# Feed-forward layer, first product: seven matmul products for eight on pairs of chunks and pairs of row blocks, with the weights' sums kept in DRAM

## The chip, the cores and the metric

The kernel runs on one core of a Trainium2 chip. A core has a matmul engine (TensorE, PE in the profile, with its weight loads as PEld), a vector engine (VectorE, DVE), a scalar engine (ScalarE, ACT), a general engine (GpSimd, POOL) and a queue engine (SyncE, SP) that issues most DMA transfers. Each engine runs its own list of instructions in order and waits on semaphores for the others. PE reads from on-chip memory (SBUF) and writes to eight accumulator banks of 128 x 512 floats (PSUM). The metric is the time of one execution on the device in microseconds; the number shown for a kernel is the median of its runs.

## What is computed

A linear attention, then a Fourier mixing, then a feed-forward layer on 8 x 576 = 4608 rows of 512 channels:

```
kv  = einsum('bhsd,bhse->bhde', k, v)
o   = einsum('bhsd,bhde->bhse', q, kv)
x   = o / sqrt(mean(o*o) + 1e-6) * g_norm
u   = x + real(fft(fft(x, seq), channels))
un  = (u - mean(u)) / sqrt(var(u) + 1e-6)
out = u + maximum(un @ w_ch1, 0) @ w_ch2
```

`w_ch1` is 512 x 2048 and `w_ch2` 2048 x 512, both in double precision in DRAM. The hidden width 2048 is cut into 16 chunks of 128, and the 4608 rows into 9 blocks of 512.

## The kernel before, in words

Every matmul of the feed-forward layer takes 128 x 128 stationary and 128 x 512 moving values. To keep float32 accuracy a value is split into a high and a low part, and a product is made of three passes (high x high, high x low, low x high). For one block and one chunk the first product takes 4 parts of the channels x 3 passes = 12 matmuls (`ffn1`, recorded at L469), and the second takes 4 row tiles x 3 passes = 12 matmuls (`ffn2`, L487). Between them ACT writes the high part of the relu (L479) and DVE the low part (L482).

The work has two stages. In the first, a planner (`Plan`) orders attention, Fourier part, and the feed-forward chunks 0 to 2 of all blocks (`plan_early`), whose sums go to the DRAM buffer `part_scr`; the transposed rows of `u`, split into high and low, go to `unT_scr`. The planner also prepares the weights of the first NA + NB1 = 7 chunks (`plan_w`). Preparing a weight chunk is a chain of DVE steps (L398 to L414, L1348, for `w_ch1` also L419 and L434), one ACT copy for the high part and one POOL subtraction for the low part.

In the second stage (from L1319) the list `segs` sets the order: the last four blocks first get chunks 3 to 6, with their sums in `next_scr`; then each block gets all the chunks that it lacks and is finished. Two loops run in it: over the segments, and in each over its chunks. Each pass of the inner loop issues the weight load of two passes ahead, `first` of this chunk, `second` of the pass before it, and the weight work of the next chunks (`sum_w`, `split_w`); when a block starts, the next block's `unT` is loaded (L1427). All prepared weights stay in SBUF. Near a block's end `load_parts` and `load_u` fetch the sums and `u`, compute the row scale (1 over the deviation) by bn_stats on DVE, and POOL adds the sums to `u` (L1418); the last chunk's accumulators are scaled, added and stored (L1456, L1461). The row scale is thus applied after both products: relu(a x) = a relu(x) for a > 0.

The instructions of this stage are not ordered by the planner but by a scheduler that works from the source's order and its own estimates, engine by engine. A tile of a pool that is used up, or whose memory another tile held before it, waits for the last reader of the old contents.

## Time and profile before

| | before |
| --- | --- |
| median of 3 runs | 1009.84 us (1007.83 to 1011.03) |
| span of the profiled execution | 1006.6 us |
| DVE busy | 488.3 us (49%) |
| ACT busy | 326.6 us (32%) |
| POOL busy | 322.2 us (32%) |
| HBM traffic | 139 GB/s over the span |

The table's lower part is from the profile's first part, the busy time of each engine in one profiled execution. Of that execution the profile gives the span from the first to the last instruction; the device time of the other runs holds a few microseconds more. In the views quoted below a row reads: line of the code, engine, operation, output tile <- input tiles, shapes, count, busy time, mean duration in ns. A row of the windows view gives, for a stretch of the span, the busy time of each engine with its count of instructions, then the granted clock of PE, the busy share of the DMA engines and what they moved.

### The profile page before, as it was taken

What the parts mean: (1) busy time and instruction counts of PE and PEld (TensorE: products, weight loads), DVE (VectorE), ACT (ScalarE), POOL (GpSimd) and SP (SyncE); (2) the same over time, 40 slices, a digit from 0 to 9 for tenths busy, and PEclk for the clock granted to TensorE, in tenths of its full rate; (3) what the DMA queues carried; (4) which work ended last, traced back from release to release, by engine and by line L of the source; (5) the groups of instructions that cost most, each with busy time, mean ns of one, the idle gap of its engine ahead of it and who ended that gap; (6) DMA issues with size and microseconds to landing.
All of it is one profiled execution on the core that took longest, in us unless ns stands there. A gap on an engine that the chain in (4) does not pass through costs nothing.

```text
span 1006.6 us, 15538 instructions
## 1 busy us (share of the span) xinstructions
PE 987.5 (98%) x6070; PEld 831.2 (83%) x6070; DVE 488.3 (49%) x946; ACT 326.6 (32%) x649; POOL 322.2 (32%) x338
## 2 busy tenths in 40 slices
PE   5999999999999999999999999999999999999998
PEld 4898889888878788888888888888888888888886
DVE  3588986778598689995131323221221311311212
ACT  2566655756544333444121212021021120210110
POOL 1557786785674132227440303020120020200000
PEclk9999999999999999999999999999999999999999
DMA  9889876873555865646642423320410400400101
GB/s 232 206 211 285 208 221 190 223 207 124 192 185 163 301 222 209 230 126 200 207 147 96 124 98 112 120 90 1 167 43 1 168 21 1 167 0 1 42 1 42
DMA packets 109405, 140.48 MB, mean 140 GB/s; under 512 B 51870, under 2 KB 77010, under 8 KB 104724
## 3 DMA queue, kind: packets, MB, share of 16 engines
q1 hardware_dynamic: 105652, 131.89, 42.9%
q0 software_dynamic: 1920, 6.29, 2.1%
q10 hardware_dynamic: 1760, 1.31, 0.5%
q8 instruction: 48, 0.79, 0.3%
q14 instruction: 25, 0.20, 0.1%
HBM read 88.07 MB, written 51.40 MB: 139 GB/s over the span
## 4 chain that ended last, share of the span: by engine, by line
PE 95%; DVE 3%; issue 1%; DMA 0%; POOL 0%; ACT 0%; DVEq 0%; POOLq 0%; ACTq 0%
PE ps_h L469 38%; PE acc L487 38%; PE ps_o L748 4%; PE ps_f L902 4%; PE ps_k L653 2%; PE ps_f L962 2%; PE ps_s L542 2%; PE ps_q L722 2%; PE ps_t L1063 1%; PE ps_w L428 1%; DVE x L853 1%; DMA raw<-in_moe_w_ch_dram 0%; DVE pm L991 0%; DVE ab L865 0%; DVE x L1007 0%
## 5 line engine op out<-in xcount | busy, mean ns | idle before, releaser
L469 PE MATMUL ps_h<-unTh,w 128*128 128x512 f32 x1152 | 356.6, 391 | 0.0
L487 PE MATMUL acc<-w,hh 128*128 128x512 f32 x1152 | 345.7, 391 | 0.0
L482 DVE SCALAR_TENSOR_TENSOR hl<-ps_h,hh 128x512 fp32r<-128x512 f32 x144 | 99.2, 689 | 376.3 <-ACT hh L479 372.1
L469 PEld LDWEIGHTS ps_h<-unTh,w 128*128 128x128 f32 x1152 | 215.0, 188 | 44.0
L487 PEld LDWEIGHTS acc<-w,hh 128*128 128x128 f32 x1152 | 214.6, 188 | 43.9 <-ACT unTh L1072 0.2
L479 ACT ACTIVATE hh<-ps_h 128x512 fp32r<-128x512 f32 x144 | 85.9, 597 | 475.5 <-PE ps_h L469 455.9
L469 PE MATMUL ps_h<-unTl,w 128*128 128x512 f32 x576 | 224.2, 389 | 0.0
L487 PE MATMUL acc<-w,hl 128*128 128x512 f32 x576 | 213.3, 390 | 0.0
L487 PEld LDWEIGHTS acc<-w,hl 128*128 128x128 f32 x576 | 108.1, 188 | 22.7
L469 PEld LDWEIGHTS ps_h<-unTl,w 128*128 128x128 f32 x576 | 108.0, 188 | 22.6
L1399 POOL DMA_INDIRECT uu<-u_scr,rowidx x24 | 23.4, 977 | 285.2 <-DVE uu L1456 177.6
L788 POOL TENSOR_TENSOR x<-x,gb 96x512 f32<-96x512 f32 (+1 forms) x42 | 53.7, 1299 | 32.9 <-ACT x L765 21.7
L1418 POOL TENSOR_TENSOR uu<-uu,up 128x512 f32<-128x512 f32 x36 | 45.7, 1295 | 45.7 <-ACT up L1415 45.7
L1362 POOL TENSOR_TENSOR w<-wap,w 128x512 fp32r<-128x512 f32 x18 | 23.3, 1295 | 70.0 <-ACT w L1361 70.0
L1456 DVE SCALAR_TENSOR_TENSOR uu<-acc,rs_yb,uu 128x512 f32<-128x512 f32 (+1 forms) x37 | 25.4, 730 | 41.1 <-PE acc L487 41.1
L748 PEld LDWEIGHTS ps_o<-kvt,fq 64*96 64x96 f32 (+1 forms) x864 | 38.9, 162 | 5.9 <-issue 1.4
L748 PE MATMUL ps_o<-kvt,fq 64*96 64x64 f32 (+1 forms) x864 | 42.2, 248 | 0.9 <-DVE x L853 0.6
L775 DVE TENSOR_REDUCE ss<-ps_o 96x8 f32<-96x512 f32 (+1 forms) x48 | 32.4, 685 | 21.7 <-ACT ps_o L770 21.6
L875 POOL TENSOR_TENSOR xe<-ab 96x256 f32<-96x256 f32 (+1 forms) x46 | 34.5, 770 | 25.6 <-DVE ab L865 22.6
L902 PE MATMUL ps_f<-cs,xh 96*128 96x290 f32 (+1 forms) x192 | 39.5, 300 | 0.0
L1406 DVE BATCH_NORM_STATS2 bst<-uu 128x6 f32<-128x512 f32 x36 | 24.5, 687 | 25.8 <-DMA uu<-u_scr,rowidx 17.6
L1075 DVE TENSOR_TENSOR unTl<-ps_t,unTh 128x384 fp32r<-128x384 f32 (+14 forms) x80 | 33.0, 472 | 2.8 <-ACT unTh L1072 2.8
(125 smaller groups left out, 1035.8 us busy)
## 6 DMA issues: line engine op xcount, KB each, us to landing
raw<-in_moe_w_ch_dram SPq DMA_DIRECT2D x32, 512.0 KB
unT_scr<-unTh SPq DMA_DIRECT2D x9, 1024.0 KB
unT_scr<-unTl SPq DMA_DIRECT2D x9, 1024.0 KB
part_scr<-part SPq DMA_DIRECT2D x36, 256.0 KB
unTh<-unT_scr SPq DMA_DIRECT2D x9, 1024.0 KB
unTl<-unT_scr SPq DMA_DIRECT2D x9, 1024.0 KB
up<-part_scr SPq DMA_DIRECT2D x36, 256.0 KB
out_dram<-uu SPq DMA_DIRECT2D x35, 256.0 KB
```

Of the source, the lines that this page charges most:

```text
L469: nc.tensor.matmul(ps, w[c][:, kc * P : (kc + 1) * P], unT[a][:, kc, :], start=(idx == 0), stop=(idx == 3 * KC - 1),)
L479: nc.scalar.activation(hh, ps, AF.Relu)
L482: nc.vector.scalar_tensor_tensor(hl, ps, 0.0, hh.bitcast(F32), ALU.max, ALU.subtract)
L487: nc.tensor.matmul(acc, hpair[a][:, i * P : (i + 1) * P], w[c], start=(first and n == 0), stop=(last and n == 2),)
L748: nc.tensor.matmul(pss[s].t[:n, at : at + D], fqs[side].t[half, m, :n], kvt.t[half, m], start=True, stop=True,)
L775: nc.vector.tensor_reduce(ss.t[0][:n, :, t, s::2], pss[s].t[:n].rearrange("p (u m e) -> p u m e", u=2, e=D), AX.X, ALU.add,)
L788: nc.gpsimd.tensor_tensor(v_, v_, gb[:n].unsqueeze(1).to_broadcast([n, H, D]), ALU.mult)
L875: nc.gpsimd.tensor_tensor(o[:, s], a[:, 0], a[:, 1], ALU.subtract if s else ALU.add)
L902: nc.tensor.matmul(ps.t[:, :NS], xs[t].t[a][:n, part, ch * P : (ch + 1) * P], cs[:n, part, c, t, :], start=(idx == 0), stop=(idx == 8),)
L1075: nc.vector.tensor_tensor(unTs[j].t[1][:, :, to], view()[:, :, lo:hi], unTs[j].t[0][:, :, to].bitcast(F32), ALU.subtract,)
L1418: nc.gpsimd.tensor_tensor(us[j][i], us[j][i], part, ALU.add)
L1456: nc.vector.scalar_tensor_tensor(ut[:, cols], acc_t[i][:, cols], scales[j][:, i : i + 1], ut[:, cols], ALU.mult, ALU.add,)
```

## The change

NB1 becomes 3: six chunks are prepared in the first stage, and all blocks do chunks 3 to 5 in the ordinary way in the second. Block 0 (`LONE`) alone does chunks 6 to 15 in the ordinary way, two at a time, between the segments of the other blocks. While that runs, the weights of chunks 6 to 15 are prepared in five groups of two. For each group the 512 x 256 piece of `w_ch1` is seen as 2 x 2 quarters of 256 channels x 128 hidden values; POOL makes four sums and differences of quarters (Winograd's form of Strassen's scheme), all are split into high and low, and the seven resulting operands go to `w1_scr` in DRAM, the `w_ch2` pieces to `w2_scr`.

Then all pools of the second stage are closed and a third stage begins, for the other eight blocks in four pairs. For a pair, `prep_u` fetches `u` of the two blocks and computes the row scale, `prep_z` loads high and low of `unT`, adds them and multiplies by the row scale (fetched through `scale_scr` so that it lies along the free axis), `prep_t` makes the four sums of the 2 x 2 quarters, `prep_b` splits the seven operands, and `prep_acc` adds the earlier sums to `u`. The main loop runs 4 pairs x 5 groups = 20 times. Each time it loads the group's weights again, does seven products of 6 matmuls (`mult`, two parts of the channels x three passes) in place of eight, combines them by DVE adds and ACT copies in PSUM and SBUF, makes the relu, and does the second product for both blocks of the time before (`outputs`, 2 x 24 matmuls), which DVE adds to `u` after every group. The preparation of the next pair is spread over the loop's passes.

```diff
-NB1 = 4
-NSEG = 4
+NB1 = 3
...
+    def split_into(hi, lo, src, eng=None):
+        nc.scalar.activation(hi, src, AF.Copy)
+        (eng or nc.gpsimd).tensor_tensor(lo, src, hi.bitcast(F32), ALU.subtract)
...
+        a11, a12, a21, a22 = up[:, :HK], up[:, HK:], af[:, :HK], af[:, HK:]
+        sc = work.tile([P, 4, HK], F32, name="wsc", tag="wsc", bufs=1)
+        nc.gpsimd.tensor_tensor(sc[:, 0], a21, a22, ALU.add)
+        nc.gpsimd.tensor_tensor(sc[:, 1], sc[:, 0], a11, ALU.subtract)
+        nc.gpsimd.tensor_tensor(sc[:, 2], a11, a21, ALU.subtract)
+        nc.gpsimd.tensor_tensor(sc[:, 3], a12, sc[:, 1], ALU.subtract)
...
+        nc.sync.dma_start(
+            w1_scr[g], t[:, :7].rearrange("p q c n -> p (q c n)").bitcast(F32)
+        )
...
+    segs = [(NBLK - 2, first_fs), (NBLK - 1, first_fs), (LONE, first_fs)]
+    for g in range(NG):
+        segs.append((LONE, [F1 + 2 * g, F1 + 2 * g + 1]))
+        if g < NG - 1:
+            segs.append((rest.pop(0), first_fs))
+    segs += [(j, first_fs) for j in rest]
...
+    left.close()
     late.close()
     qkv_ctx.close()
...
+    def prep_u(p):
+        for j in PAIRS[p]:
+            us[j], scale_of[j] = fetch_block(
+                j, lambda: usp[p % 2].tile([P, DM], F32, name="us", tag="us", bufs=2 * TPB)
+            )
+            nc.sync.dma_start(
+                scale_scr[j : j + 1].rearrange("o (i p) -> p (o i)", p=P), scale_of[j]
+            )
+
+    def prep_z(p):
...
+            nc.sync.dma_start(wide, scale_scr[j].partition_broadcast(P))
...
+                nc.sync.dma_start(t, unT_scr[j, :, 0, cols])
+                nc.sync.dma_start(low, unT_scr[j, :, 1, cols])
+                nc.gpsimd.tensor_tensor(t, t, low, ALU.add)
...
+                nc.gpsimd.tensor_tensor(
+                    tv, tv, wide.unsqueeze(1).to_broadcast([P, 2, BT]), ALU.mult
+                )
+
+    def prep_t(p):
...
+        nc.gpsimd.tensor_tensor(z["z1"], z["z12"], z["z11"], ALU.subtract)
+        nc.gpsimd.tensor_tensor(z["z2"], z["z22"], z["z1"], ALU.subtract)
+        nc.gpsimd.tensor_tensor(z["z12"], z["z22"], z["z12"], ALU.subtract)
+        nc.gpsimd.tensor_tensor(z["z4"], z["z21"], z["z2"], ALU.subtract)
+
+    def prep_b(p, m):
...
+        split_into(t[:, 0], t[:, 1], zs[p][Z_OF[name]], nc.vector)
+
+    def prep_acc(p, which):
...
+                part = up2.tile([P, DM], F32, name="up2", tag="up2", bufs=3)
+                nc.sync.dma_start(part, src[n * P : (n + 1) * P])
...
+            nc.gpsimd.tensor_tensor(two_[0], two_[0], two_[1], ALU.add)
+            add_part(j, i, us[j][i], two_[0], scale_of[j])
...
+    prep_u(0)
+    load_w1c(0)
+    prep_z(0)
+    prep_t(0)
+    for m in (1, 6, 5, 7, 2, 4, 3):
+        prep_b(0, m)
+    load_w2c(0)
+    prep_acc(0, 0)
+    prep_acc(0, 1)
+
+    load_w1c(1)
+    load_w2c(1)
...
+        mult(a, 1, n, True, False)
+        s1 = s_tile()
+        nc.scalar.copy(s1, a)
+        turn_over(1)
+        d = bank("ps_h")
+        mult(d, 6, n, True, False)
+        s2 = s_tile()
+        add_ps(s2, d, s1)
...
+        outputs(n - 1, 0)
+        mult(a, 2, n, False, True)
...
```

What this makes of the engines' lists is shown at the seam between the second and the third stage. On PE the second stage was one unbroken row of the two products; these are PE's last rows before the program's end (`ps_h` is the first product's bank, `acc` the second's, `unTh` and `unTl` the block's rows, `w` a weight):

```order
L469 MATMUL ps_h<-unTl,w_5797 128x512
L469 MATMUL ps_h<-unTh,w_5797 128x512 x2
L469 MATMUL ps_h<-unTl,w_5797 128x512
L487 MATMUL acc<-w_5748,hh 128x512 x2
L487 MATMUL acc<-w_5748,hl 128x512
```

Behind these rows come only more of the second product.

Now, at the end of the second stage, PE has the last `second` of block 1 and then the first products of the third stage (`b` and `t` are the split operands; b_6774 is `b11`, b_6786 `b21`, t_6777 `t2`, t_6780 `t1`, t_6783 `t3`):

```order
L1452 MATMUL acc<-w_4803,hh 128x512 x8
L1452 MATMUL acc<-w_4803,hl 128x512 x4
L1652 MATMUL ps_h<-b_6774,w1c 128x512 x6
L1652 MATMUL ps_h<-b_6786,w1c 128x512 x6
L1652 MATMUL ps_h<-t_6777,w1c 128x512 x2
L1652 MATMUL ps_h<-t_6780,w1c 128x512 x6
L1652 MATMUL ps_h<-t_6777,w1c 128x512 x4
```

Nothing of the second stage stands behind block 1 any more; after the products of `b11` and `b21` the next ones read `t2` and `t1`.

On SP a block's start before was the next `unT`, the stores of the finished block, and the fetch of `u` and of the sums:

```order
L1427 DMA unTh<-unT_scr 128x2048
L1427 DMA unTl<-unT_scr 128x2048
L1461 DMA out_dram<-uu 128x512 x4
L1397 DMA uu<-u_scr 128x512
L1384 DMA up<-part_scr 128x512 x4
```

Now SP has at the seam, behind the first three of the four stores of block 1's sums and the first load of `prep_acc` (`lp` are these sums, `up` the tiles of `prep_acc`, `us` those of `u`, `rs_yb` the row scale):

```order
L1635 DMA up_6799<-next_scr 128x512
L1635 DMA up_6804<-part_scr 128x512
L1514 DMA next_scr<-lp 128x512
L1642 DMA w1c<-w_scr 128x3584
L1646 DMA w2c<-w_scr 128x2048
L1460 DMA us<-u_scr 128x512 x4
L1642 DMA w1c<-w_scr 128x3584
L1646 DMA w2c<-w_scr 128x2048
L1635 DMA up_6806<-next_scr 128x512
L1635 DMA up_6811<-part_scr 128x512
L1592 DMA scale_scr<-rs_yb 128x4x1
L1600 DMA wide<-scale_scr 128x512
```

The loads of the weights of two groups stand ahead of and behind the loads of `u`, and the store and the load of the row scale stand behind all of them and behind two more loads of `prep_acc`.

On POOL a block before was the additions of its two sums where it has two (L1387), its fetches of `u`, and four additions to `u`:

```order
L1387 TENSOR_TENSOR up<-up 128x512 x4
L1399 DMA uu<-u_scr,rowidx 128x512 x3
L1418 TENSOR_TENSOR uu<-uu,up 128x512 x4
L1387 TENSOR_TENSOR up<-up 128x512 x3
L1399 DMA uu<-u_scr,rowidx 128x512 x3
```

None of these is waited for by PE's next product.

Now POOL has, behind the four additions of high and low (L1608) of the first pair and the fetches of six tiles of `u` of the second pair (z_6741 is `z11`, z_6747 `z21`, z_6755 `z12`, z_6761 `z22`, z_6767 `z1`, z_6768 `z2`), these rows, in two fences without a gap between them:

```order
L1637 TENSOR_TENSOR up_6797<-up_6797,up_6799 128x512
L1462 DMA us<-u_scr,rowidx 128x512 x6
L1637 TENSOR_TENSOR up_6804<-up_6804,up_6806 128x512
L1488 TENSOR_TENSOR us<-us,up_6797 128x512
L1488 TENSOR_TENSOR us<-us,up_6804 128x512
L1610 TENSOR_TENSOR z_6741<-z_6741,wide 128x1024
L1610 TENSOR_TENSOR z_6747<-z_6747,wide 128x1024
L1637 TENSOR_TENSOR up_6811<-up_6811,up_6813 128x512
L1610 TENSOR_TENSOR z_6755<-z_6755,wide 128x1024
L1610 TENSOR_TENSOR z_6761<-z_6761,wide 128x1024
L1488 TENSOR_TENSOR us<-us,up_6811 128x512
```

It goes on with

```order
L1637 TENSOR_TENSOR up_6818<-up_6818,up_6820 128x512
L1618 TENSOR_TENSOR z_6767<-z_6755,z_6741 128x1024
L1488 TENSOR_TENSOR us<-us,up_6818 128x512
L1637 TENSOR_TENSOR up_6825<-up_6825,up_6827 128x512
L1619 TENSOR_TENSOR z_6768<-z_6761,z_6767 128x1024
```

The additions for `prep_acc` (L1637, L1488) stand among the steps that make `z11`, `z1` and `z2`.

More of the change, by code (lines that the diff above doesn't have):

```diff
@@ L1390, in load_u @@
[L1390 to L1404 removed]
+        g, r = divmod(f - F1, 2)
@@ new lines @@
+    units = [(which, F1 + 2 * g + r) for g in range(NG) for which in (1, 2) for r in range(2)]
+    rest = [j for j in range(NBLK - 1, -1, -1) if j not in (NBLK - 2, NBLK - 1, LONE)]
+    first_fs = list(range(NA, F1))
+    segs = [(NBLK - 2, first_fs), (NBLK - 1, first_fs), (LONE, first_fs)]
[4 more added lines that the diff above has]
+    segs += [(j, first_fs) for j in rest]
+    acc_t = {}
@@ new lines, with load_unT, relu, first @@
+    lone = {}
+    loaded = [NBLK - 2, NBLK - 1]
+    def load_unT(j):
+        loaded.append(j)
+        if j == LONE:
+            unTs[j] = [extra.tile([P, KC, BT], F32R, name=f"un{c}") for c in "hl"]
+        else:
+            unTs[j] = unT_tiles()
+        for c in range(2):
+            nc.sync.dma_start(unTs[j][c].rearrange("p c t -> p (c t)").bitcast(F32), unT_scr[j, :, c])
+    def relu(ps, hpair):
+        relu_hi(hpair[0], ps)
+        relu_lo(hpair[1], ps, hpair[0])
+    def first(j, f):
+        ps = bank("ps_h")
+        idx = 0
+        for kc in range(KC):
+            for a, c in passes:
+                nc.tensor.matmul(
+                    ps, w1_of(f, c, kc), unTs[j][a][:, kc, :],
+                    start=(idx == 0), stop=(idx == 3 * KC - 1),
+                )
+                idx += 1
+        hpair = h_tile("hh"), h_tile("hl")
+        relu(ps, hpair)
+        return hpair
@@ new lines, in product, with fetch_u @@
+    def product(acc, hpair, f, i, first_, last_):
+        for n, (a, c) in enumerate(passes):
+            nc.tensor.matmul(
+                acc, hpair[a][:, i * P : (i + 1) * P], w2_of(f, c),
+                start=(first_ and n == 0), stop=(last_ and n == 2),
+            )
+    def fetch_u(j, i, ut):
+        n = j * TPB + i
+        if ascending(n):
+            nc.sync.dma_start(ut, u_scr[n * P : (n + 1) * P])
+        else:
+            nc.gpsimd.indirect_dma_start(
+                out=ut,
+                out_offset=None,
+                in_=u_scr[:NTOK],
+                in_offset=bass.IndirectOffsetOnAxis(ap=rowidx[:, n : n + 1], axis=0),
+            )
@@ L1472 @@
                 load_w(*units[step + 2])
-            if f == f0 and n + 1 < len(segs) and segs[n + 1][0] not in held:
-                load_unT(segs[n + 1][0], j)
+            if f == fs[0]:
+                ahead = next((k for k, _ in segs[n + 1 :] if k not in loaded), None)
+                if ahead is not None:
+                    load_unT(ahead)
             hpair = first(j, f)
@@ new lines @@
+    h2 = pool("h2")
+    s1p = pool("s1p")
+    up2 = pool("up2")
+    usp = {1: pool("us1")}
+    bop = pool("bop")
+    zop = pool("zop")
+    lop = pool("lop")
+    sop = pool("sop")
+    wcp = {0: pool("wc0")}
+    usp[0] = pool("us0")
+    wcp[1] = pool("wc1", side="right")
+    B_OF = {1: "b11", 2: "b21", 3: "b22", 4: "t4", 5: "t1", 6: "t2", 7: "t3"}
+    A_OF = {1: 0, 2: 1, 3: 6, 4: 2, 5: 3, 6: 4, 7: 5}
+    Z_OF = {"b11": "z11", "b21": "z21", "b22": "z22", "t1": "z1", "t2": "z2", "t3": "z12", "t4": "z4"}
@@ new lines, in load_w2c, with mult @@
+    def load_w2c(n):
+        t = w2c[n] = wcp[n % 2].tile([P, 2, 2, BT], F32R, name="w2c", tag="w2c")
+        nc.sync.dma_start(t.rearrange("p f c n -> p (f c n)").bitcast(F32), w2_scr[n % NG])
+    def mult(ps, m, n, fresh, done):
+        b, w, idx = bs[B_OF[m]], w1c[n], 0
+        for kc in range(2):
+            for a, c in passes:
+                nc.tensor.matmul(
+                    ps,
+                    w[:, A_OF[m], c, kc * P : (kc + 1) * P],
+                    b[:, a, kc * BT : (kc + 1) * BT],
+                    start=(fresh and idx == 0),
+                    stop=(done and idx == 5),
+                    skip_group_check=True,
+                )
+                idx += 1
```

320 lines of the change are left out of this document (218 added, 102 removed).

## The prediction

> **What bounds the kernel now.** I read the page's busy times first, then the chain that ended last, then windows of the second stage, then the chain in order of time.
>
> ```profile
> span 1006.6 us, 15538 instructions
> PE 987.5 (98%) x6070; PEld 831.2 (83%) x6070; DVE 488.3 (49%) x946; ACT 326.6 (32%) x649; POOL 322.2 (32%) x338
> PE 95%; DVE 3%; issue 1%; DMA 0%; POOL 0%; ACT 0%; DVEq 0%; POOLq 0%; ACTq 0%
> ```
>
> PE holds 95% of the chain that sets the end. A busy PE alone would not prove that, since overlapping matmuls count as busy; the share of the chain does.
>
> ```profile
> 700.00:750.00 50.00, 50.00 (x223) 41.39 (x222) 12.67 (x26) 8.41 (x14) 7.90 (x7) 1.00 0.31 106
> 402.78 5.45 PE acc L487 x24
> ```
>
> In the window, PE is busy for all 50 us while DVE, ACT and POOL work for 12.67, 8.41 and 7.90 us, and the DMA engines for 31% of the time. 24 matmuls take 5.45 us, so one costs 0.227 us. In the second stage a matmul removed is worth its 0.227 us, as long as nothing makes PE stand still.
>
> **The change part by part.**
>
> *Matmuls.* A pair and a group have 2 blocks x 2 chunks x 12 = 48 first-product matmuls before and 7 x 6 = 42 after. Over 4 pairs x 5 groups that is 20 x 6 = 120 fewer: 120 x 0.227 = **27.3 us less** on PE. The second product, block 0 and chunks 0 to 5 keep their numbers.
>
> *The seam between the second and the third stage.* Before, the next block's products always stood behind the current one's. In PE's new list the last `second` of block 1 is followed at once by the products of `b11` and `b21`, and then by those of `t2`. So I follow what these wait for, from T, the end of block 1's last matmul. Can the preparation be done before T? Only in part: the `z` loads and the POOL additions of high and low stand ahead of block 1's stores. The row scale doesn't: on SP its store and its load stand behind the stores of block 1's sums, which exist only after T, behind all the weights' loads, and behind `up_6811`, which needs POOL's addition of `up_6804` and `up_6806`. SP really stands still for its head:
>
> ```profile
> SPq L1427 <- PE ps_h L469: 201.3, 8, 46.4
> ```
>
> So all of this must land after T: four stores, four loads of `prep_acc`, four loads of `us` on SP and six on POOL (18 x 128 x 512 x 4 bytes = 4.72 MB), and twice w1c and w2c (128 x 3584 and 128 x 2048 floats, 2.88 MB each time), together 10.5 MB. The rate and the latency come from these rows:
>
> ```profile
> 715.10:721.10 6.00, 6.00 (x28) 4.99 (x27) 1.12 (x2) 0.60 (x1) 0.00 (x0) 1.00 0.92 348
> 723.50:729.50 6.00, 6.00 (x28) 4.99 (x27) 1.93 (x4) 0.60 (x1) 2.86 (x3) 1.00 0.84 295
> L1281 SPq DMA_DIRECT2D p_scr<-p0u x1: 264/264/264, 294.1 to 294.1; - x1
> L1285 SPq DMA_DIRECT2D p0r<-p_scr x1: 289/289/289, 296.4 to 296.4; - x1
> L1290 PEld LDWEIGHTS ps_t<-ident,p0r x1: 134/134/134, 298.2 to 298.2; 36*128 36x128 f32 x1
> ```
>
> The last column of the first two is GB/s: 348 while two large loads run alone, 295 where stores, loads and POOL's fetches mix. A small store issued at 294.1 let its reader issue at 296.4, and PE used what it read at 298.2: 2.3 us for a store to DRAM, 1.8 us for a load. I take 348, since most of the bytes are large rows: 10.5 MB / 348 = 30.1 us, and 35.5 at 295. With ACT's copy of the accumulator ahead (0.60), the issue and the load's latency, `up_6806` is there at about T + 33.2. The rest goes by these rows:
>
> ```profile
> L1418 POOL TENSOR_TENSOR uu<-uu,up 128x512 f32<-128x512 f32 x36 | 45.7, 1295 | 45.7 <-ACT up L1415 45.7
> L571 POOL TENSOR_TENSOR cs<-draw,cs 97x870 fp32r<-97x870 f32 x2 | 4.1, 2062 | 0.1
> L568 ACT ACTIVATE cs<-draw 97x870 fp32r<-97x870 f32 x2 | 1.9, 938 | 0.0
> L1448 ACT COPY up<-acc 128x512 f32<-128x512 f32 x16 | 8.2, 600 | 6.0 <-PE acc L487 6.0
> ```
>
> POOL takes 1.30 us for 512 columns and 2.06 for 870. Operations of 1024 columns don't occur; the line through the two gives 2.39 on POOL, bounded by 2.06 below and 2 x 1.30 = 2.59 above. For ACT I take 1.05 between 0.94 and 1.20 in the same way. Then: POOL's addition 1.3 (T + 34.5), SP's issues 0.35, store of the scale 2.3, its broadcast load 1.8 and 0.75 for its 262 KB (T + 39.7), POOL's multiplication of `z11` 2.39, ACT's high part 1.05: PE starts `b11` at **T + 43**. On POOL, from the end of that multiplication (T + 42.1) to the end of `z2`, the order has five operations of 1024 columns (z21, z12, z22, z1, z2) and five of 512 for `prep_acc`: 5 x 2.39 + 5 x 1.30 = 18.5, so T + 60.6, and ACT's 1.05 makes it **T + 61.7** for `t2`. In between PE has 12 matmuls, 2.7 us. It loses 61.7 - 2.7 = **59.0 us**. Behind that, 42 products (9.5 us) cover the way to `t4`.
>
> Its bounds: at 295 GB/s 5.4 us more, and POOL at 2.59 instead of 2.39 for six operations 1.2 more: 66. At the low end the weights' loads delay nothing: POOL issues its last fetch of `u` about 12 us after T (one takes about 1 us of POOL), it arrives 3.4 us later by
>
> ```profile
> 724.04 0.96 POOL L1399 DMA_INDIRECT uu<-u_scr,rowidx  x1 [55.89 <-DVE uu L1456]
> 727.45 0.69 DVE L1406 BATCH_NORM_STATS2 bst<-uu 128x6 f32<-128x512 f32 x1 [0.92 <-DMA uu<-u_scr,rowidx]
> ```
>
> and statistics, scale and the DRAM round trip take some 8 us: T + 23, then 2.39 + 1.05 + 18.5 + 1.05 less 2.7: 43 us. I take 59, since in-order SP gives no way around `up_6806`.
>
> *PE's restart.* After such a pause the first matmuls are slower:
>
> ```profile
> 13.62 2.05 PE L542 MATMUL ps_s<-still 128*128 128x512 f32 x4
> 21.73 0.95 PE L542 MATMUL ps_s<-still 128*128 128x512 f32 x3
> ```
>
> Four cost 2.05 us after the idle start; three cost 0.95 some microseconds later, so four would cost about 1.2. That is 0.9 us; the first restart is hidden by the wait for `t2`, the second counts: **0.9**, between 0 and 2. The Trainium skill, page "TensorE: Matmul & The Clock Gate", Part 1, says that an idle window of about 3.4 us halves PE's clock and that it takes as long a busy window to restore it; by it the estimate is 1.7 us in place of 0.9, and the sum would be 1043. The profile's granted clock reads 1.00 in the windows of the second stage, in which PE never idles, so it neither shows nor denies this.
>
> *The second stage.* Its PE work per chunk is the same. DVE gets 20 weight units where 18 were, and additions for block 0. Is it still covered? Near it was tight:
>
> ```profile
> 380.00:405.00 25.00, 25.00 (x114) 20.77 (x113) 24.47 (x43) 10.96 (x19) 6.12 (x5) 1.00 0.66 231
> 409.12 1.28 DVE L408 SCALAR_TENSOR_TENSOR ps_a<-raw,ps_a 128x512 uint32<-128x512 uint32 x2
> 410.32 0.68 DVE L411 TENSOR_SCALAR wap<-ps_a 128x512 uint32<-128x512 uint32 x1
> ```
>
> Two DVE operations start 1.20 us ahead of the third, so one costs 0.60 when packed and 0.68 alone. Twenty units x 6, ten x 1.7 us for `w_ch1`'s mean, 21 relus and some 8 additions make 106 us at 0.60 and 119 at 0.68; PE's 21 chunks take 114. So 0 to 5 us; I take 0, with the packed spacing, at which PE didn't wait before.
>
> *The third stage's loop.* A pass has 90 matmuls, 20.4 us. DVE has 16 operations of 512 columns (4 combining, 4 relu, 8 additions), at most 16 x 0.69 = 11.0 us, and where a pair turns over seven of 1024 columns more, at most 9.7. The combining chain for `t4` and `b22` lies under 24 matmuls of `outputs`. So PE covers it; bounds 0 and 1 us a turn. The DMA engines are closer: a pair's five passes load 14.4 MB of weights and 13.1 MB for the next pair and the output, 27.5 MB in 102 us, 269 GB/s, below 295. I take 0; the price if not is the second rival.
>
> *Sum.* 1006.6 - 27.3 + 59.0 + 0.9 = 1039.2 us of span. The median of the runs, 1009.84, is 3.2 over the profiled span; with the same offset, **1042 us**.
>
> **The rivals.**
>
> *The seam is covered: faster.* If the first pair's `u` and scale were made during block 1's segment, PE would go on at once: 1006.6 - 27.3 + 3.2 = 983. It decides at a seam of 27 us. For it: the DMA engines have room (31% in the window above) and the `z` loads do come early. Against it: the row scale's place on SP behind block 1's stores, and 23 us of POOL, ACT and POOL again that stand behind the scale in any case. 5%.
>
> *Transfers bind the loop.* If the mixed rate falls to 250 GB/s, a pair's 27.5 MB take 110 us instead of 102, 8 us at each of three turns, and the seam 12 us more: 1042 + 36 = 1078; half of it, 1060, is as likely. For it: 295 in a mixed window; against it: 348 in a plain one. 13%.
>
> *The weights don't delay the scale.* A seam of 43 us: 1026. For it: POOL's fetches don't come from SP's queue. Against it: `up_6811`. 10%.
>
> *The saving isn't there.* If each pass made PE wait one product of 6 matmuls (1.4 us) for the combining, the 27 us would be gone: 1069. Against it: the 24 matmuls in between. 2%.
>
> **How the numbers follow.** My forecast, 1042, has 70%, within about 1035 to 1052. The range reaches to the short seam at 1026, and up to 1068, which takes in 66 us of seam, 5 in the second stage, and half of what the transfers could cost. About 0.3% is what a measurement of this kernel can tell from no change, 3 us: faster 0.05, within 0.02, slower 0.93.
>
> **What would show it.** Right: one stretch of about 45 us without matmuls near 60% of the span, 12 matmuls, and a second one of some 15 us; the DMA share near 1 in the first; in the second POOL at work throughout; first product matmuls 120 fewer; no further gap over 2 us in the loop. Wrong: a seam below 27 us; PE windows of the loop with fewer than 220 matmuls in 50 us; or gaps where pairs turn over.

## The result, and the profile after

The changed kernel takes **1116.7 us** (median of 4 runs, 1113.42 to 1117.69) where the kernel before takes 1010.43 in the runs beside it: a ratio of **1.105**, 95% interval 1.1035 to 1.1069. It is slower, as forecast, but by more than three times as much: 106 us where 32 were predicted. The first rows of the new page are the span and the busy times:

```profile
span 1114.9 us, 16128 instructions
PE 984.7 (88%) x5950; PEld 819.4 (73%) x5950; DVE 686.0 (62%) x1198; ACT 392.7 (35%) x747; POOL 500.1 (45%) x434
...
PEclk9999999999999999999985579999889998899999
...
PE 62%; DMA 19%; DVE 7%; POOL 6%; issue 4%; ACT 1%; SPq 0%; POOLq 0%; DVEq 0%; ACTq 0%
```

The 120 matmuls are gone (6070 before, 5950 now), but PE's share of the chain that sets the end fell from 95% to 62%, and transfers hold 19% of it. The row of the granted clock dips at the seam (slices 21 to 24 of 40) and twice more behind it.

The windows view says where PE stands. Its rows give the stretch in us, then PE, PEld, DVE, ACT and POOL busy with counts, then the clock, the DMA share and GB/s. For the kernel after:

```profile
330.00:573.00 243.00, 236.44 (x1048) 194.34 (x1046) 146.41 (x226) 81.65 (x144) 85.56 (x73) 1.00 0.71 255
573.00:652.00 79.00, 6.96 (x14) 4.15 (x15) 24.81 (x53) 12.03 (x18) 37.19 (x24) 0.53 0.54 174
...
700.00:960.00 260.00, 230.39 (x947) 185.02 (x946) 148.71 (x231) 65.23 (x103) 134.07 (x81) 0.94 0.69 229
```

Of the 79 us of the seam PE works for 7. In the 260 us of the loop in which the next pairs are prepared it lacks 30 us and its clock is 0.94. Before, this half of the program read

```profile
560.00:1006.00 446.00, 442.62 (x1953) 366.18 (x1951) 97.25 (x186) 66.74 (x111) 42.63 (x38) 1.00 0.19 64
```

**One account for all kernels.** From the starts of successive matmuls I count two kinds of loss. A step of over 0.75 us is a *gap*, and costs what it has above 0.227. A step of 0.32 to 0.75 us is a *slow step*, again counted above 0.227. Block 1's last matmul ends at T = 572.8. In us, for the second stage (330 to 560), the seam (560 to 700) and the rest of the third stage (from 700):

| kernel | second stage: gaps / slow | seam: gaps / slow | loop: gaps / slow |
| --- | --- | --- | --- |
| before | 1.2 / 0.0 | 0.0 / 0.0 | 0.0 / 0.0 |
| after | 7.0 / 0.2 | 78.0 / 6.5 | 31.1 / 13.7 |

Gaps grew by 114.9 us and slow steps by 20.4. The matmuls' own time behind 330 us, that is the sum of all steps without these losses, fell from 671.2 to 644.3, by 26.9. Together that is +108.4; the spans differ by 108.3 (1114.9 - 1006.6). Of the seam's 78.0 us of gaps 73.6 lie ahead of `t2` and 4.4 at `t4`.

The timeline of PE shows the two pauses (start, duration, line, tiles, count, and in brackets the idle time before and what ended it):

```profile
571.76 1.07 PE L1452 MATMUL acc<-w,hl 128*128 128x512 f32 x4
624.36 1.22 PE L1652 MATMUL ps_h<-b,w1c 128*128 128x512 f32 x2 [51.54 <-ACT b L1360]
...
651.26 6.01 PE L1652 MATMUL ps_h<-t,w1c 128*128 128x512 f32 x14 [18.90 <-ACT t L1360]
```

The chain of waits in order of time (start, duration, what held it; pieces under 0.4 us left out) says what the first one is made of:

```profile
589.14 16.04 DMA up<-next_scr
605.32 1.27 POOL up L1637
607.02 8.89 DMA scale_scr<-rs_yb
615.98 4.77 DMA wide<-scale_scr
```

The first scale, 2 KB, takes 8.9 us from the issue of its store to the issue of its load, and the load 4.8. The second block's scale follows in SP's timeline:

```profile
617.34 0.38 SPq L1592 DMA_DIRECT2D scale_scr<-rs_yb  x1
628.63 0.32 SPq L1600 DMA_DIRECT2D wide<-scale_scr  x1
```

Its store takes 11.3 us, for which SP stands still. POOL's timeline shows who waits:

```profile
633.92 4.63 POOL L1610 TENSOR_TENSOR z<-z,wide 128x1024 f32<-128x1024 f32 x2 [6.16 <-DMA wide<-scale_scr]
```

POOL is idle 6.16 us, and as `t2` needs POOL's next four steps of `z` (L1610 twice, L1618, L1619), it comes as much later. During the first store no bandwidth is short, as the second of two rows of the windows view shows:

```profile
573.00:607.00 34.00, 0.00 (x0) 0.00 (x0) 9.46 (x30) 2.77 (x6) 10.20 (x11) 0.53 0.87 334
607.00:616.00 9.00, 0.00 (x0) 0.00 (x0) 3.99 (x14) 0.94 (x4) 2.03 (x2) 0.50 0.14 29
```

Up to T + 34 the DMA engines move 334 GB/s; during the first store 29 GB/s, at a share of 0.14. SP's waits give the sum over the eight blocks (total us, times, longest):

```profile
SPq L1600 <- DMA scale_scr<-rs_yb: 70.9, 8, 10.8
```

About twenty of these 71 us belong to the first pair, ahead of `t2`; the other fifty belong to the later pairs and lie in the loop's passes.

The store holds up more than its reader. The chain of waits around one pause of the loop starts with a store of the scale (L1592) and the load that SP issues 0.5 us behind it (pieces under 0.1 us left out):

```profile
812.55 0.37 SPq L1592
813.02 12.05 DMA up<-next_scr
825.23 1.26 POOL up L1637
826.52 0.81 ACT up L1485
827.33 0.48 ACT s L1741
827.86 2.93 PE ps_h L1652 x6
```

This load of 256 KB lands after 12.05 us, 1.3 us behind the store itself. POOL's addition waits for it, ACT's next step (L1485) for POOL, and ACT's copy of a product's accumulator (L1741), for which PE stands still, comes behind that on ACT. The pause that ends at 947.49 has the same rows, with 12.43 us for a load issued 1.2 us behind a store, and the gap at `t4` hangs on a load of `z`, issued 0.4 us behind the third store, that takes 14.15 us. The other pauses of the loop were not traced to their cause.

### The profile page after: what moved, and what is told of

Read it like the earlier page. It is cut to its first block, busy times and chain, and to the rows that moved or that the text cites. A ratio compares the mean times of both kernels' runs of the same rounds, so it can differ in the third digit from the quotient of the medians.

```text
span 1114.9 us, 16128 instructions
## 1 busy us (share of the span) xinstructions
PE 984.7 (88%) x5950; PEld 819.4 (73%) x5950; DVE 686.0 (62%) x1198; ACT 392.7 (35%) x747; POOL 500.1 (45%) x434
## 4 chain that ended last, share of the span: by engine, by line
PE 62%; DMA 19%; DVE 7%; POOL 6%; issue 4%; ACT 1%; SPq 0%; POOLq 0%; DVEq 0%; ACTq 0%
PE acc L1685 12%; PE ps_h L1652 9%; DMA up<-next_scr 7%; PE acc L493 6%; PE ps_h L475 6%; PE ps_h L1441 6%; PE acc L1452 6%; PE ps_o L754 4%; PE ps_f L908 4%; DMA us<-u_scr,rowidx 2%; PE ps_k L659 2%; PE ps_f L968 2%; DMA next_scr<-lp 2%; POOL up L1637 2%; DMA z<-unT_scr 2%
## 5 line engine op out<-in xcount | busy, mean ns | idle before, releaser
L1685 PE MATMUL acc<-w2c,hh 128*128 128x512 f32 x640 | 202.7, 399 | 11.1 <-issue 11.1
L1652 PE MATMUL ps_h<-b,w1c 128*128 128x512 f32 x360 | 97.6, 408 | 62.6 <-ACT b L1360 51.5
L1685 PEld LDWEIGHTS acc<-w2c,hh 128*128 128x128 f32 x640 | 123.7, 194 | 39.2 <-issue 12.6
L1652 PE MATMUL ps_h<-t,w1c 128*128 128x512 f32 x480 | 123.7, 408 | 32.3 <-ACT t L1360 18.9
L1652 PEld LDWEIGHTS ps_h<-t,w1c 128*128 128x128 f32 x480 | 94.1, 198 | 55.8 <-ACT t L1360 19.6
L1695 DVE TENSOR_TENSOR us<-acc,us 128x512 f32<-128x512 f32 (+1 forms) x161 | 106.4, 679 | 38.2 <-PE acc L1685 37.5
L1652 PEld LDWEIGHTS ps_h<-b,w1c 128*128 128x128 f32 x360 | 70.1, 197 | 80.5 <-ACT b L1360 52.0
L1685 PE MATMUL acc<-w2c,hl 128*128 128x512 f32 x320 | 126.6, 396 | 0.0
L1637 POOL TENSOR_TENSOR up<-up,up 128x512 f32<-128x512 f32 x32 | 46.8, 1463 | 62.3 <-DMA up<-next_scr 50.7
L1485 ACT ACTIVATE up<-up,p0c,rs_yb 128x512 f32<-128x512 f32 x32 | 25.9, 814 | 127.0 <-POOL up L1637 122.1
L493 PE MATMUL acc<-w,hh 128*128 128x512 f32 x216 | 67.6, 399 | 0.0
L475 PE MATMUL ps_h<-unTh,w 128*128 128x512 f32 x216 | 67.6, 394 | 0.0
L1452 PE MATMUL acc<-w,hh 128*128 128x512 f32 x216 | 61.3, 390 | 0.0
L1441 PE MATMUL ps_h<-unTh,w 128*128 128x512 f32 x192 | 59.5, 391 | 1.4 <-DVE wa L1354 1.4
L1608 POOL TENSOR_TENSOR z<-z,low 128x1024 f32<-128x1024 f32 x16 | 39.9, 2493 | 39.0 <-DMA z<-unT_scr 28.5
L1610 POOL TENSOR_TENSOR z<-z,wide 128x1024 f32<-128x1024 f32 x16 | 38.7, 2437 | 38.0 <-DMA wide<-scale_scr 28.8
```

Of the source, the lines that this page charges most:

```text
L475: nc.tensor.matmul(ps, w[c][:, kc * P : (kc + 1) * P], unT[a][:, kc, :], start=(idx == 0), stop=(idx == 3 * KC - 1),)
L493: nc.tensor.matmul(acc, hpair[a][:, i * P : (i + 1) * P], w[c], start=(first and n == 0), stop=(last and n == 2),)
L1441: nc.tensor.matmul(ps, w1_of(f, c, kc), unTs[j][a][:, kc, :], start=(idx == 0), stop=(idx == 3 * KC - 1),)
L1452: nc.tensor.matmul(acc, hpair[a][:, i * P : (i + 1) * P], w2_of(f, c), start=(first_ and n == 0), stop=(last_ and n == 2),)
L1637: nc.gpsimd.tensor_tensor(two_[0], two_[0], two_[1], ALU.add)
L1652: nc.tensor.matmul(ps, w[:, A_OF[m], c, kc * P : (kc + 1) * P], b[:, a, kc * BT : (kc + 1) * BT], start=(fresh and idx == 0), stop=(done a ...
```

## The experiments

The question was what the 78 + 31 us of gaps and the 20 us of slow steps hang on. The theory: the trip of the row scale through DRAM, whose store is made of 512 pieces of 4 bytes and whose wait blocks SP. Its rivals: the mass of transfers; the clock after pauses; DVE and POOL work in the loop. Ratios are to the kernel before, run beside each.

### The scale spread by PE in place of DRAM

```diff
-            nc.sync.dma_start(
-                scale_scr[j : j + 1].rearrange("o (i p) -> p (o i)", p=P), scale_of[j]
-            )
...
-            nc.sync.dma_start(wide, scale_scr[j].partition_broadcast(P))
+            ps = bank("ps_s")
+            for i in range(TPB):
+                nc.tensor.matmul(
+                    ps[:, i * P : (i + 1) * P],
+                    scale_of[j][:, i : i + 1].to_broadcast([P, P]), ident,
+                    start=True, stop=True,
+                )
+            nc.scalar.copy(wide, ps)
```

> The row scale no longer goes through DRAM: four matmuls of 128 columns spread it over the partitions, ACT copies the result; nothing else is edited. Theory A (the store of 512 scattered values of 4 bytes, 8.9 us and 11.3 us where 2.3 was reckoned, and the loads behind it, make the seam longer than reckoned, and SP, which stands 70.9 us for these stores, makes part of the loop's gaps): the first gap shrinks by about 12 us (51.7 to about 40), the two together by about 20 (73.6 to about 54), the loop's 31 us of gaps by a third or more; 1075 to 1090 us. Rival B (the scale is late because its inputs are late, since the weights' loads fill the DMA queues): the first gap stays above 47, the total above 1105. Rival C (the seam shrinks as in A, but the loop's gaps have nothing to do with the scale's stores): seam 54, loop gaps unchanged at about 31; 1093 to 1100 us.

1062.45 us, ratio 1.052 (1.0503 to 1.0538): 54 us less than the changed kernel, better than expected. Gaps and slow steps are 52.5 / 5.9 at the seam and 4.2 / 1.5 in the loop. So the trip costs some 25 us at the seam, **and nearly all of the loop's loss**: 27 of 31 us of gaps and 12 of 14 of slow steps. The work of DVE and POOL in the loop stays (172 and 123 us of the stretch from 700 to 960, where it was 149 and 134), so that work doesn't make the loop's gaps. PE's waits of this run show what is left at the seam: the scale itself, with all but 0.8 us of the first row, then `t2`.

```profile
PE ps_s L1599 <- DVE rs_yb L456: 38.3, 3, 29.9
PE ps_h L1656 <- ACT t L1360: 12.5, 1, 12.5
```

### The scale applied to the outputs

`z` is not scaled; the scale multiplies the second product when it is added, as in the kernel before.

```diff
-            wide = sop.tile([P, BT], F32, name="wide", tag="wide", bufs=2)
-            nc.sync.dma_start(wide, scale_scr[j].partition_broadcast(P))
...
-                tv = t.rearrange("p (c t) -> p c t", c=2)
-                nc.gpsimd.tensor_tensor(
-                    tv, tv, wide.unsqueeze(1).to_broadcast([P, 2, BT]), ALU.mult
-                )
...
-                nc.vector.tensor_tensor(ut[:, cols], ps[:, cols], ut[:, cols], ALU.add)
+                nc.vector.scalar_tensor_tensor(
+                    ut[:, cols], ps[:, cols], scale_of[j][:, i : i + 1], ut[:, cols],
+                    ALU.mult, ALU.add,
+                )
```

> z is not multiplied by the row scale at all; the scale is applied where the second product is added to u (relu(s x) = s relu(x) for s > 0), so the result is the same. Theory A (the seam is the chain of the scale): without it the first product waits for w1c[0] alone, whose place in SBUF overlaps the last stores of block 1: about T + 13, both gaps together about 15 us in place of 73.6, no second gap; the gap of 4.4 for t4 goes; POOL loses 16 operations of 2.4 us. 1025 to 1050 us. Rival B (the seam is the 10.5 MB of transfers): the first product at T + 30 or later, 1070 or more. Rival D (DVE stands in order for the first pair's u, whose statistics stand ahead of the first combining): first product at T + 13, but a new gap of 10 to 25 us within the first pass; 1040 to 1065.

1035.09 us, ratio 1.0256 (1.0232 to 1.028). In the loop there is no gap and no slow step at all, although all the loads of `z`, `u`, sums and weights are still made:

```profile
700.00:990.00 290.00, 290.00 (x1261) 236.57 (x1261) 194.24 (x299) 79.51 (x124) 95.89 (x61) 1.00 0.63 229
```

That rules out the mass of transfers for the loop: 229 GB/s here without a loss, the same 229 with one in the changed kernel. So the total lies where it was expected, but the seam does not: it keeps 37.4 us where about 15 were expected. Its cause is new: the first product no longer needs the scale, and its weights are late.

```profile
PE ps_h L1646 <- DMA w1c<-w_scr: 33.1, 1, 33.1
```

### PE kept busy through the seam

208 and 70 matmuls that nothing reads stand in the two pauses; the first three products of the first pass are written ahead.

```diff
+    def spin(k_, w, x):
+        ps = bank("ps_s")
+        for k in range(k_):
+            nc.tensor.matmul(ps, w, x, start=(k == 0), stop=(k == k_ - 1))
+
+    spin(208, prev[1][0][:, :P], prev[1][0])
...
+        mult(a, 2, 0, False, True)
+        spin(70, w1c[0][:, 0, 0, :P], w1c[0][:, 0])
```

> As the changed kernel, with 208 matmuls of 512 columns to a spare bank behind the last matmul of block 1 (47 us, inside the 51.7 us gap) and 70 more (16 us, inside the 19.3 us gap) between the products of b21 and t2. They compute nothing that is used. Theory A (a matmul after a pause takes up to twice as long because PE stood still): the 22 slow steps behind the two gaps (5.0 us above 0.227 each) nearly vanish, the first t2 product starts where it did (about T + 79), the span is 3 to 6 us shorter; the loop's slow steps stay. Rival (the slow steps come from what else is busy, such as transfers and POOL): slow steps as before, span the same within 1 us.

1105.76 us in one run, span 1104.0. That is 10.9 less where at most 6 were expected, so this expectation missed. The scheduler had also put both scale stores ahead, so that `t2` came at 641.25 instead of 651.26, and the total tells nothing of the clock alone. The windows do:

```profile
573.00:652.00 79.00, 78.33 (x346) 64.56 (x345) 37.84 (x59) 14.46 (x22) 41.59 (x22) 1.00 0.59 193
```

The clock is 1.00 where it was 0.53, and the slow steps of the seam fall from 6.5 to 1.8 us; those of the loop, whose gaps stay (33.0), stay as well (11.8). Slow steps follow pauses, and go with them.

### Where the first weights of the third stage lie

Made on the kernel with the scale at the outputs: the pools of `w1c` and of `u` change places.

```diff
-    wcp = {0: pool("wc0")}
     usp[0] = pool("us0")
+    wcp = {0: pool("wc0")}
```

> As the one with the scale at the output, and two pools of the third stage change places, so that w1c[0] no longer overlaps the buffers from which block 1's sums are stored (the first pair's u does, in part). Theory A: w1c[0] is there before T, the first product starts right behind block 1's last matmul, the seam is below 5 us and the total about 10 us below the kernel with the scale at the output alone. Rival D (DVE stands for the first pair's u): the gap moves into the first pass and the total is within 4 us of the other. Rival B (transfers): no gain either, with a gap at the first product.

1034.97 us, ratio 1.0252 (1.0235 to 1.0269): no gain. The gap of 33 us still waits for `w1c`. The exchange missed its aim, since the new place still lay over buffers of block 1's sums. SP's timeline also shows the first group's `w1c` (598.63) behind the second group's (581.56), and both behind four `z` loads that took 11.37 us to issue:

```profile
566.68 11.37 SPq L1604 DMA_DIRECT2D z<-unT_scr  x4
...
581.56 0.97 SPq L1636 DMA_DIRECT2D w1c<-w_scr  x1
...
598.63 0.32 SPq L1636 DMA_DIRECT2D w1c<-w_scr  x1
```

### First weights in free memory, first loads in a fixed order

On the kernel with the scale at the outputs: `w1c` and `u` of the first group get memory that the second stage has done with; SP takes the first loads in the written order; `low` comes in halves, and `w2c` and two of the split operands get pools of their own. All this was changed at once, so no single share is known.

```diff
+    usp[0] = pool("us0")
     bop = pool("bop")
...
+    bop2 = pool("bop2")
+    wdp = {0: pool("wd0")}
...
+    def first_loads():
+        prep_z(0)
+        load_w1c(0)
+        prep_u(0)
+        load_w2c(0)
+        load_w1c(1)
+        load_w2c(1)
+
+    plan.in_line(nc.sync, first_loads)
```

> As e2 (scale at the output), and the inputs of the first pass are fetched early: w1c[0] and the first pair's u lie where buffers of block 0 and of the weights lay, not where block 1's sums are stored from, and SP issues w1c[0] ahead of w1c[1], the next pair's z and block 1's stores; low comes in halves (three buffers of 512 columns), and the tiles b21 and b22 take the place behind. Theory A: e2's gap of 33 us ahead of the first product is the wait for w1c[0] alone; it falls below 5 us. The statistics of u and the sums of chunks 0 to 5 still stand ahead of the first pass on DVE and POOL, and may stop it. If u lands by T (573), the total is 1000 to 1006; theory D (DVE, in order, stands for u, or the first outputs wait for POOL's sums): 10 to 20 us of the gap come back within the first two passes, 1010 to 1025. Rival B (the transfers' rate sets the time): gap and total as e2, 1030 or more.

1018.44 us, ratio 1.0081 (1.0054 to 1.0107). The gap ahead of the first product is gone; the seam has 15.7 us in five small gaps, and 8.2 of slow steps.

### Sums and statistics later

The same, with the statistics of `u` behind the first pass on DVE, `prep_acc` in the own pair's second pass, and the next pair's `u`, `z` and `t` one pass later.

```diff
-    prep_acc(0, 0)
-    prep_acc(0, 1)
...
+        if n == 0:
+            stats(0)
+        if g == 1:
+            prep_acc(p, 0)
+            prep_acc(p, 1)
         if more:
-            if g == 0:
+            if g == 1:
                 prep_u(p + 1)
...
+    plan.in_line(nc.vector, lambda: one(0))
```

> As e5, and the statistics of u stand behind the first pass's combining on DVE, the sums of chunks 0 to 5 are added in the second pass of their own pair in place of the fourth pass of the pair before, and the next pair's u, z and t are fetched and made one pass later. Theory A and D: no gap over 3 us behind T; the third stage at 0.227 to 0.230 us a matmul throughout: span about 330 + 242 + 1840 matmuls x 0.229 = 993 to 1000, total 996 to 1003, faster than the kernel before (1010). Rival: the later preparation makes a new wait at each turn of the pairs, three times 3 to 8 us: 1010 to 1025.

1016.54 us, ratio 1.0061 (1.0037 to 1.0085): not told apart from the run before it, and short of the expectation. The gaps stayed where they were (17.5 at the seam, 2.7 in the loop). Here the transfers do bind, for a short stretch: the next pair's loads had moved ahead of the first group's own.

```profile
570.00:575.00 5.00, 4.07 (x17) 2.73 (x15) 1.23 (x1) 0.43 (x1) 4.37 (x4) 1.00 1.00 340
...
595.00:600.00 5.00, 3.00 (x7) 2.17 (x8) 2.36 (x2) 2.00 (x2) 1.98 (x2) 0.50 1.04 425
```

The copy of block 1's sums for `next_scr` also waited 7.0 us for a buffer.

### The whole loop in the written order

```diff
-            part = lone_pool.tile([P, DM], F32, name="lp", tag="lp", bufs=3)
+            part = lone_pool.tile([P, DM], F32, name="lp", tag="lp", bufs=6)
...
-    plan.in_line(nc.sync, first_loads)
+    plan.in_line(nc.sync, lambda: plan.in_line(nc.gpsimd, first_loads))
...
+    plan.in_line(nc.sync, lambda: plan.in_line(nc.vector, all_passes))
```

`prep_acc` and `prep_z` are also spread over more passes.

> As e6, and the order that the scheduler chose is replaced by a written one in the third stage: SP and DVE follow the program there, POOL makes the first pair's z and t before it fetches u, the next pair's z and u and the sums of chunks 0 to 5 are spread over the passes (at most 5.8 MB a pass, 284 GB/s), and block 1's sums get six store buffers in place of three. Theory A (what is left behind T in e6, 17.5 us of gaps and 8.5 us of slow steps, is early loads for the next pair, 6 MB, that stand ahead of the first pair's own on the same queues, and one copy that waits for a store buffer): gaps behind T below 6 us, slow steps below 3, span 992 to 1000, total 995 to 1003. Rival (the first pair's own inputs, some 12 MB behind 545, cannot come sooner at about 400 GB/s): 12 us of gaps or more stay, total 1008 to 1018. Rival (written orders make new waits in the loop): the loop's gaps, 2.7 us in e6, exceed 8.

1042.56 us, ratio 1.0338 (1.0305 to 1.0371): worse. Half of its gaps, 21.2 us, now lie in the loop, because DVE and SP keep an order that doesn't fit (of the second row 2.7 us lie in the loop, the rest before):

```profile
PE ps_h L1665 <- DVE ps_h L1682: 18.0, 3, 6.3
PE ps_h L1665 <- DMA w1c<-w_scr: 9.8, 6, 2.6
```

### Only the seam in order

From the kernel with late sums, with the last run's fixed order at the seam alone: POOL and SP in order for the first loads, six `lp` buffers, and the next pair's loads and the sums behind them on SP; two other split operands (`t4`, `b22`) get the separate pool.

```diff
+    def behind_first(emit):
+        start = len(tc.nc.cur_bb.bb.instructions)
+        emit()
+        for i in on_sp(start):
+            tc.add_manual_dep(
+                i, first_done,
...
         if g == 1:
-            prep_acc(p, 0)
-            prep_acc(p, 1)
+            behind_first(lambda: (prep_acc(p, 0), prep_acc(p, 1)))
```

> As e6, with e7's edits at the seam alone: POOL makes the first pair's z and t ahead of its fetches of u, six store buffers for block 1's sums, the next pair's loads and the sums of chunks 0 to 5 stand on SP behind the first pair's own loads, and t4 and b22 (not b21 and b22) lie where block 1's sums are stored from. SP and DVE keep the scheduler's order in the loop. Theory A (e7's loss is the written order of SP and DVE in the loop, its seam was better than e6's): gaps and slow steps behind T as e7's seam or less (15 us up to 640, against 26 in e6), loop as e6 (3 us): 1000 to 1010. Rival (the first pair's inputs bind): no better than e6, 1014 to 1018.

**998.77 us, ratio 0.9891 (0.9874 to 0.9907)**: faster than the kernel before, and better than expected. Its page has

```profile
PE 966.6 (97%) x5950; PEld 808.8 (81%) x5950; DVE 691.9 (70%) x1206; ACT 391.6 (39%) x747; POOL 463.8 (47%) x434
```

and two of its windows are

```profile
573.00:652.00 79.00, 74.06 (x307) 58.87 (x306) 53.23 (x110) 23.56 (x41) 50.18 (x39) 0.96 0.89 344
...
700.00:990.00 290.00, 289.28 (x1275) 238.53 (x1274) 191.26 (x298) 78.56 (x123) 87.69 (x66) 1.00 0.59 212
```

PE works for 74 of the 79 us that were the seam. Left are 4.5 / 5.0 there, 0.5 / 0.8 in the loop and 5.5 / 0.4 in the second stage: 16.7 us, less the 1.2 of before. Taken from the 27.2 that the matmuls save this gives 11.7; the spans differ by 11.5 (1006.6 - 995.1).

### The scale still through DRAM, but in rows

Made on the changed kernel: PE transposes the scale, and the store has 4 pieces of 512 bytes instead of 512 pieces of 4. Place and readers stay.

```diff
-            nc.sync.dma_start(
-                scale_scr[j : j + 1].rearrange("o (i p) -> p (o i)", p=P), scale_of[j]
-            )
+            ps = bank("ps_s")
+            nc.tensor.transpose(ps[:TPB, :P], scale_of[j], ident)
+            row = sop.tile([TPB, P], F32, name="row", tag="row", bufs=2)
+            nc.scalar.copy(row, ps[:TPB, :P])
+            nc.sync.dma_start(scale_scr[j].rearrange("(i p) -> i p", p=P), row)
```

> As the changed kernel, with one edit: the row scale (128 partitions x 4) is turned by PE to 4 x 128 and stored as four rows of 512 bytes, where the changed kernel stores 512 single values of 4 bytes; the broadcast load stays. Theory A (it is the number of small pieces that makes the store long): SP's waits ahead of the broadcast load fall from 8 to 11 us each to 2 to 4, the seam from 73.6 to about 60, and the loop's gaps of 31 us fall by half or more: 1070 to 1090 us. Rival B (the store is long since the queues are full when it is issued): 7 us or more each, total above 1105. Rival C (the loop's gaps don't hang on the store): store short, loop gaps still about 31, 1098 to 1105.

The store did what it should. SP's timeline:

```profile
605.67 0.26 SPq L1596 DMA_DIRECT2D scale_scr<-row  x1
606.95 0.32 SPq L1602 DMA_DIRECT2D wide<-scale_scr  x1
609.29 0.26 SPq L1596 DMA_DIRECT2D scale_scr<-row  x1
611.22 0.32 SPq L1602 DMA_DIRECT2D wide<-scale_scr  x1
```

From store to load it is now 1.3 and 1.9 us instead of 8.9 and 11.3. The total missed all the same: 1121.94 us, ratio 1.1116 (1.1098 to 1.1135). The transposes stand in PE's list where the statistics are made, a pass ahead of the scale's use, and PE, which works in order, stands still until the scale is there:

```profile
PE ps_s L1593 <- DVE rs_yb L456: 87.4, 7, 29.7
```

Gaps in the loop are 46.5 us. The probe had put a new wait on the bound engine.

### The same rows, transposed one pass later

```diff
     def prep_z(p):
+        z = zs[p] = {}
+        for s_, j in enumerate(PAIRS[p]):
+            ps = bank("ps_s")
+            nc.tensor.transpose(ps[:TPB, :P], scale_of[j], ident)
...
+            nc.sync.dma_start(scale_scr[j].rearrange("(i p) -> i p", p=P), row)
             wide = sop.tile([P, BT], F32, name="wide", tag="wide", bufs=2)
```

> As the kernel with the scale stored in four rows (e9), whose store became short (1.3 and 1.9 us in place of 8.9 and 11.3 at the seam) but whose transposes stood in PE's order ahead of scales that came late (46.5 us of gaps behind 665, all at the transposes). Here PE turns the scale only where z is made, one pass later. Theory A (a short store takes the loop's gaps away, e9's were the transposes' own): gaps behind 665 below 15 us, seam as e9 (about 60 to 70 with the clock), total 1070 to 1090. Rival (the loop's gaps come from the loads of wide and z, whatever the store): gaps behind 665 of 25 us or more, total above 1095.

1065.46 us, ratio 1.054 (1.0517 to 1.0562): 51 us less than the changed kernel, with the same 2 KB a block still going through DRAM and back. Seam 63.3 / 5.4, loop 6.1 / 1.6. So the pieces of 4 bytes are the cause and not the trip as such; that is nearly what taking the trip away gained (54). The store stands a pass later here for the later pairs, but in the run before, where its place was the old one, SP's waits for it had fallen already, from 70.9 us to 7.4 (here 1.6). A load of sums issued at 608.33, 0.4 us behind a row store, is at POOL by 611.19. At the seam `b11` starts at T + 43.0 and `t2` at T + 65.9. The row store changes the size and the number of the pieces together; which of the two counts wasn't tried.

### Weight units split a step later

On the fastest kernel: a weight unit is split two steps after its load, for the second stage's gaps. With it the sums of weights get one buffer more (five) and `lp` one less (five).

```diff
-            if 0 < step <= len(units):
-                split_w(*units[step - 1])
+            if 1 < step <= len(units) + 1:
+                split_w(*units[step - 2])
```

> As e8, with one edit in the second stage: a weight unit is split (and its mean taken on PE) two steps after its loading in place of one, so that PE's mean no longer stands ahead of products for a sum that DVE has not finished; one more buffer for a sum, one less for block 1's stores. Theory (the 5.5 us of gaps between 330 and 560, e8, are these in-order waits): they fall below 2.5 us (1.2 stand at 331 ahead of the stage's units), total 993 to 997. Rival (DVE's load itself, 43 operations of 24.5 us in 25 us of a tight window, sets the pace): gaps only move, 997 to 1000.

997.83 us, ratio 0.9867 (0.9844 to 0.9891): the interval overlaps with that of the run it started from. The second stage's gaps went from 5.5 to 4.0 us, above the expected bound of 2.5. Inconclusive in time, and so is which of the three edits did it.

## Why the prediction was right in sign and wrong in size

- *What bounds the kernel; 120 matmuls fewer, 27.3 us less.* Right: the matmuls' own time fell by 26.9. The sign is no luck either: the two pauses of the seam alone cost 73.6 us.
- *`up_6806` is there at about T + 33.2.* Right: its transfer ended at 605.2, T + 32.4. So the rival in which the weights don't delay the scale falls, and so does that of the covered seam.
- *"Store of the scale 2.3, its broadcast load 1.8 and 0.75."* **This step failed.** They took 8.9 and 4.8 us, 8.8 more than the 4.85 summed, and that is all of the first product's delay (T + 51.6 for T + 43). The price had come from a store of full rows; the store priced with it has one 4-byte piece for each value, which stands in the code (`"o (i p) -> p (o i)"`). With rows of 512 bytes it measured 1.3 to 1.9 us at the seam, below the 2.3 taken.
- *`t2` at T + 61.7.* Mis-sized, T + 78.5. The sum counted one store. The second block's came behind it on in-order SP, 11.3 us, and POOL waited. Of the 16.8 us, 8.3 were lost up to the end of `z11`, 6.2 are this wait, and 2.2 are POOL's ten operations up to `z2`, 20.7 us where 18.5 was summed. Most of these had the predicted length (2.38 us is the median of L1610, for 2.39), but three lasted about 1 us longer, and why is open. With the store in rows `b11` starts at T + 43.0 for the predicted T + 43, `t2` at T + 65.9 for T + 61.7, and the seam's gaps are 63.3 us for the predicted 59.0; that this is so near is in part luck, as that run has PE's transposes in the path.
- *"42 products (9.5 us) cover the way to `t4`."* **Failed**, at 4.4 us: POOL's subtraction for `t4` (L1621) stands behind an addition for the next pair (L1608), which waited 9.1 us for the load of `z` held up behind the third store.
- *The loop: "So PE covers it … I take 0."* **Failed**, at 31.1 us. The step compared the sums of work of each engine and the bytes, and these do fit: without the scale's trip the same loads leave no gap. What it left out is the store of the scale: SP waits for it for each block, 50 us in the loop, and a load issued right behind it is held up too (12 us and more, where a load next to a row store took about 3). Two of the six pauses over 2 us follow from such a load by the chain shown above; how the others follow was not traced, and that they go with the store is shown by the runs without it.
- *The rival "transfers bind the loop".* It named the right places, the turns from pair to pair, and would have been nearer (1078), but its mechanism is wrong: the loop moves 229 GB/s with gaps and without.
- *PE's restart, 0.9.* Mis-sized: 20.2 us from the seam on, against none before. Two pauses were counted; there were sixteen, and one costs more. From the start of `t2`, 14 matmuls took 6.01 us, 2.8 more than at 0.227. These windows cover that restart:

```profile
651.20:657.20 6.00, 5.94 (x15) 4.75 (x16) 3.91 (x3) 1.07 (x2) 1.23 (x1) 0.54 0.26 18
657.20:660.00 2.80, 2.80 (x14) 2.31 (x13) 0.98 (x2) 1.09 (x2) 0.00 (x0) 1.00 0.63 89
```

The clock is near half for about 6 us of work and then whole. In the loop it reads 0.50 behind each of the six pauses of 3 to 6 us (the first row is behind the second of them), and 1.00 from 700 to 779, where the four pauses were of 0.9 to 1.5 us:

```profile
813.90:817.10 3.20, 3.20 (x9) 2.49 (x8) 2.91 (x5) 0.00 (x0) 0.81 (x1) 0.50 0.24 16
700.00:779.00 79.00, 75.51 (x327) 60.60 (x326) 44.25 (x59) 23.84 (x36) 49.43 (x28) 1.00 0.76 267
```

The Trainium skill's rule on this (page "TensorE: Matmul & The Clock Gate", Part 1: half the clock after an idle window, whole again after a busy window of some 3.4 us) agrees in kind, and so does the run that kept PE busy, with its clock of 1.00. Recovery behind `t2` took longer than one such window; the same page of the Trainium skill adds that the windows run freely, so a restart may meet part of one first.

- *The second stage, 0, bounds 0 to 5.* 5.8 us more gaps, just past the bound: DVE's preparation of weights is not fully covered.
- *What would show it.* The first pause was 51.5 us for 45, the second 18.9 for 15. The DMA share was 0.87 up to T + 34 and 0.14 during the first store, where near 1 was named for the whole. In the second pause POOL worked throughout but for its first 1.6 us, the end of the 6.16 us. Seven gaps over 2 us lie behind `t2`, where none was expected.

By account, the 75.7 us between the predicted span (1039.2) and the measured one are 14.6 at the seam, 35.5 at `t4` and in the loop, 19.5 of slow steps, 5.8 in the second stage, and 0.4 in the matmuls, to 0.1. Some 51 of them are the 4-byte store, by the last run with rows.

## What to carry to other kernels

Price a DMA by its contiguous pieces, read from its access pattern, and never by a neighbouring store that has other pieces. A short store whose reader is issued by the same in-order queue costs its latency on everything behind it, and a load issued between the two can be held up with it, so look for both in a loop as well, not just where they first occur. A seven-for-eight scheme pays only when the new operands' inputs are at hand: here the same arithmetic is 10.5% slower or 1.1% faster, by where the scale is applied, where the first weights lie, and in which order the first loads are issued.

## What the runs showed of the hardware

- Storing 2 KB in 512 pieces of 4 bytes took 8.9 and 11.3 us at the seam until its reader could be issued (8.2 to 11.3 over the eight stores), in 4 pieces of 512 bytes 1.3 to 1.9 us there, with the DMA engines 14% busy during the first. Three loads issued 0.4 to 1.2 us behind a store of 4-byte pieces landed after 12.05 to 14.15 us, 1.3 to 4.7 us behind it, while the DMA engines moved 47 to 73 GB/s. The Trainium skill, page "DMA: Bandwidth & Descriptors", section "Specifications", puts the least size of an efficient transfer at 512 B and says that a read-modify-write happens below it; the trace agrees that such pieces are dear, and no run here shows by what mechanism.
- A restart after a pause of 18.9 us cost 2.8 us in slow matmuls, over about 6 us at a clock of 0.54. In the loop of the changed kernel pauses of 3 to 6 us were enough to bring the clock to 0.50, and pauses of 0.9 to 1.5 us left it at 1.00: 13.7 us of slow steps beside 31.1 us of gaps.
